# First products copied from bank to bank as the start of a second chain, block 6's first layer by seven products, left tokens in plane order, and a new order of the work

## The chip, the cores and the metric

The kernel runs on one core of a Trainium2 chip. A core has TensorE (PE in the profile; PEld is its weight load), VectorE (DVE), ScalarE (ACT), GpSimd (POOL) and SyncE (SP), which issues most transfers. They run at once, each in its own fixed order, and wait for each other through semaphores. SBUF is the working memory; PSUM, in eight banks, takes what matmuls put out. The metric is the device time of one execution in microseconds, lower is better.

## What is computed

```python
def _attn_ref(q, k, v):               # q, k, v: 8 x 8 x 576 x 64
    q_d, k_d, v_d = means over 4 neighbouring positions
    out_up = np.repeat(sm_attn(q_d, k_d, v_d), 4, axis=2)
    mask = np.abs(pos[:, None] - pos[None, :]) < 4
    out_local = softmax of the masked scores, times v
    return out_up + out_local

def _moe_ref(x, w_in, w_out):         # x: 4608 x 512; w_in: 512 x 2048; w_out: 2048 x 512
    h = x @ w_in
    g = h - np.tanh(h)
    return g @ w_out
```

The attention's output, 512 wide for each of 4608 tokens, goes through two dense layers with x - tanh(x) between them.

## The kernel before

**Tiling.** There are 8 batches ("blocks" 0 to 7) of 576 tokens. Attention works on pairs of heads, four pairs to a block, 32 pairs in all. A pair's queries and keys are loaded (`st`), cast (`qr`), turned, scored on PE with 64 rows (L691, L701, L707), put through exp on ACT (`E`), masked on DVE (L747), multiplied with the values (L761), normalized on DVE (`r` L777, `ln` L779), turned back and joined into `xT` (L797). A block's dense layers take 512 of its tokens; the other 64, the "left" ones, of two blocks at a time form groups of their own (`left1`, `left2`, `left_pair`).

**First layer.** For blocks 0 to 6 it is `mm1` (L838): for each of 16 chunks of the hidden width four matmuls of 128x512, tanh on ACT (L850), a subtract on DVE into `gT` (L853). For block 7 it is `first7`, a fast 2x2 scheme: seven products of quarters instead of eight, with sums of weights (`SS`, L872, in seats of `st`) and of tokens (`XS`, L883, in `rr` and `rT`), for four groups of chunks (L949). Each product has 16 matmuls of 128x256.

**Second layer.** For blocks 1 to 7 it is such a scheme too (`product`, L1277; seven products, with `token_sums` L1212 on DVE and `weight_sums` L1186). The products come in the order 1, 2, 6, 7, 4, 5, 3 (in block 7 another one). 1 and 2 accumulate in one bank, 6, 7 and 4 in a second, 5 and 3 in a third. A result that also needs product 1 gets it from SBUF: after product 1 ACT copies the bank to `keep` (L1298), and each of three results adds it: after product 6 and after product 7 a POOL add of `keep` to the copied result (L1348), after product 4 an add on DVE that also empties the bank (L1301). `first7` does the same with its own buffers `HK` (K0: copy L932, adds L939 on POOL or DVE, L971 on DVE).

**Left tokens.** After the tanh (L1003) DVE's subtract (L1005) reorders them from (column, group) to (group, column), token by token, so that a result's 64 rows can be stored in one run.

**Order.** No scheduler decides it. Each piece of work is recorded by `op` with what it reads and writes, and four tables fix the rest: `TURNS` the order in which all pieces are put out, `ENGINES` the engine where there is a choice, `BANKS` the PSUM bank of each chain, `BEHIND` which piece on DVE or POOL waits for one on the other. Each engine runs its pieces in that order. Banks 4 to 7 are called `DENSE`, all eight `TAIL`.

```python
        if n == 1:
            copy(full[0], kept(0))
        if n in (6, 7):
            dst, keys = (ra, yk(ya, 1)) if n == 6 else (rb, yk(yb, 1))
            copy(dst, keys)
            op("POOL", 1150, lambda: GP.tensor_tensor(
                out=dst, in0=dst, in1=full[0], op=ALU.add),
               reads=[("keep", 0)], writes=keys, port=True)
        if n == 4:
            plus(y[yb][:, :, 0:HD], full[0], ("keep", 0), yk(yb, 0))
```

Of the kernel before, what the change touches and what calls it, by code (L numbers as in the profile page):

```python
# [101 lines left out]
def kernel(  # L102
# [61 lines left out]
        "7f7C6R7g4y6h3b3c7D597E72887F6i8d8e5A5u7I6k7G71896l7l6m74758E8F7H8j736n6y76778k6z966o7J6K"  # L164
        "6L977K6I6J9C7L5i5j7m8K6p5q5r7M6w6x8L7N7r7O5o5p8p78CF6M6N9D79CC7s6u6v7x9f8Q6q6r7y9g6s6t8R"
        "9Z9I9a8S8q9T9b9cCG7z9h9i7X9jCE6O6P7Y7b9k7P7Q7Z9J9l9v9w7c6SCB8v9t9u7d8w9U7V7WCD9O8x9P7R7S"
        "7eAA9m9W7h9V9X9Y7i7a7n9QCH7o7j9nAB7p7k7t70ACAD809d9o9p849eAGAd7uA1A27qAe9q9zA0AH7vA79r81"
        "7T7U9sA8BD857w82ELEMAIAh9x9y86838AAgAJ8B878GAiAjCI8H8C8MAEAM8VAFATAU8I8NAVAW8DAm8WAKAbAc"
        "Ao8J8O8ZB0B18XAL8aBGBH8fAq8PAn8gAN8Y8bBFB2B38l8h8cA9ApAk8m8iBEAt8rAOBMBIBJ8sAP8n8yAr8z8o"
        "8tDt92BcBdBN908u93AXAYBAAl91DyIgIh989EBaBbAs9FBBENEO94CJBOBPBgBh99BQ9K95Dx9AAuBiDzE09G9L"  # L170
        "9BBqEaBKBrBLE39HA5A6CLCMEJEKAv9MBsAwE4B8B9BtBRBkBlByBTEb9NE5A3A4BjE6E7BzEcEdBSCREACSCKAQ"
        "8T8UE8C0E1C1CYARBUC6CZCoE2C7C8CpBVF8BWCuC9CAEgCvEHEIASAxD0EiIcIdAyBXEhEkD2AZAaBYDuD3BZB6"
        "B7AfF7EjAzD8EPEQElEVD9ERESEeDvBmEfIeIfBuE9BvF9FAEmDEBnEBBwFDB4B5DGEnBxDHFfEwExBoDMEXEYEC"
        "IFDNEDCXEWEuEvC2F2C3ETEUDSCaFEC4BpCbBCCgIGC5F3ChFVFWFeFFCmFGFgEEEFCNFICnCTFHCUFTFUDTFBFJ"
        "COFjFkCVCcFnCPCdEoCWF4F5DFCeDUEpDwCiCQD1CjFCG7G8EqDZG1G2DaCfFZCkCqFhFiCrClFoCwCsCxDfBeBf"
        "IHFKD4G3G4CtD5CyIKDiD6CzFpFaFqDAFrIJD7DBILIMG9DIFsJxDJEGDjDKFbFcDoFtEyEzFlDpDCDODLF0F1MU"
        "DPMVG5G6DqDVIwDQ9R9SDWDDIPDbErEsDRDXDcDkIQDdDYDlDrDsFLDeFRFSJRDmGJFXFYJSEZDnGOIkIlGTFuGH"
        "GUFmFvGIHhHmGZHrINGaGcIOGhGbGuFMGAGzF6FNIqGiFdH0FwFOFPEtFxH5IuGnHAIRJ1FyFzHCIVIvHDJ2ISHI"
        "IxIyGtHNITHwHSJ3GBGCIUGsHUIiIjFQJ4HVJTJUHaG0HfJ5IIIWJ6IsItGDJ7JKJLIXIrGEHgJkJlIzHTGKGFIY"
        "GLJGJHJ8ImInGMJXGGGPJEJFJ0GQJ9K0K1GNGVJYGWGRJAGdJyGXGeGSJzJZJVGfGYJMGjK2K3JbGkGgHBJaGoHx"  # L180
        "GpDgDhGlGvIZIaK6GwGqI0K7GxI5GmJNJmJnIAJWMWGyJBJCH1H2GrJdMYH6H7JcH3K8H8K4HEJsK9HFH9MZIBH4"
        "MeHGMaMbHJJeKAICK5HKJtHHIoIpHOMfHPJoJpJfHLJgHWNAKLKMKCHXIbJqJrHMHbHQHcMrMsHYHRHiJOJPKBHj"
        "HdHZKJKKMgHkHeHnJuJvMhHoJIJJHlHsMzN0HpKuHtRDREI1HuI2HqNBMcKDI3JDNCNDM4HvKZKaNGI4M5JhJiI6"
        "I7KEKFKRKbI8KwKSMdKcI9KGKHNHKxKhNhMiL2IDIEKvJwKiKPKQKjMkKNKOKkMjJQL3L9MAKpMlLANEKqKrLPNF"
        "MmKsKtOELQMnLVMvMwNgLWMtMuN5NILbN6MBJjNiNjNJLdKILeNKLjMxMyNMNLLkNVNWL8KVNmKTKUNNLpNnHyHz"
        "KWMXNOLBLqN1N2NPLrKXN7N8LCNkKYMoMpQmLHNlLIOCLsOLNQNRNoLNOMKdNpLOKlOFOGKmNqLxMGODKnKeLcNs"
        "LyKoMJKfM3ONNbKyKgOOL4NdNeNrKzOPOHOIMKNcL0OQL5NtL6L1NTNUO7LDN9NZNaNuLEO8L7O1O2LJMqORNvLK"
        "N3N4LFLRLSLLQnLGNwNxQrOSLTLMLXNSOJLYNzO0OTOKOUMPMQQwLULfOVOWLZLgMRLlQxLhLmLaUoLtLnLiQqLu"
# [35 lines left out]
    )  # L224
    BEHIND = (
        "0211 1H12 1D1V 0z20 1t2f 5I30 5Q5N 635B 5w5W 6562 6c2x 6d6A 5u6i AACD ABCH AmAF AnAL DxC"
        "J F8CZ FfFD DFFn MUFt GAGb IrJ6 JNK7 MZJs NBKu OELA LqNn ODLO O7OQ QoNy RYOp RNR1 SURu S"
        "VRd UqUs Q0S9 UtT7 RkVM U6Vm VuW1 WJWB WIWG WWWZ WjWr XGXc XtX8 Y3Y6 YHYL YwYx ZiZj"
    )

# [1297 lines left out]
```

## Time and profile before

| what | value |
|---|---|
| time of three runs, median (lowest to highest) | 309.29 us (308.97 to 310.74) |
| span of the profiled execution | 308.9 us |
| last DVE instruction (L1046) | starts at 305.20 us, 0.42 us long |
| granted TensorE clock | 1.000 |
| first-layer matmuls, L838, 128x512 | 448 |
| first-layer matmuls by products, L949, 128x256 | 112 |
| second-layer matmuls by products, L1277, 128x256 | 1120 |
| normalizations, L779 | 32, from 16.8 us to 253.9 us |

The profile lists for each group of instructions the line, the engine, the operation, what is written and read with its shape, the count, then the busy time in us, the mean of one in ns, and the idle time of the engine before them with what ended it. A row of a stretch gives the busy time of each engine within it. One matmul's own duration (379 ns for 128x512) is longer than the distance between two, since they overlap in the array; what a stage of matmuls takes follows from the distance.

### The profile page before, as it was taken

To read this page: it belongs to the slowest core of one execution; us is meant where nothing else is said; L and a number is where in the kernel's file an instruction comes from. 1 tells how busy PE (TensorE), PEld (TensorE's weight loads), DVE (VectorE), ACT (ScalarE), POOL (GpSimd) and SP (SyncE) were. 2 spreads that over 40 slices of the span, in tenths; PEclk is the share of its full clock that TensorE was granted. 3 is DMA by queue.
4 is the path that set the end of the run, shared out by engine and by line. 5 is a ranking of instruction groups with operands and counts; after the bars stand their busy time and mean duration, and the time that the engine had idled before them with its cause. 6 is when DMAs were issued, how large, how long until landed. Compare 5 with 4: busy or idle time off the path is not lost.

```text
span 308.9 us, 8018 instructions
## 1 busy us (share of the span) xinstructions
PE 297.2 (96%) x3052; PEld 205.1 (66%) x3052; DVE 266.7 (86%) x475; ACT 221.0 (72%) x395; POOL 166.4 (54%) x227
## 2 busy tenths in 40 slices
PE   7877999999999999999999999999999999999995
PEld 2655555545577755875577765656988656889984
DVE  2677788679998988999999888999999899989995
ACT  2768686279888786988958888888789666775410
POOL 5337657026864466337872278376344766466451
PEclk9999999999999999999999999999999999999999
DMA  7999999999999999899999999989999364001215
GB/s 228 235 246 235 241 241 172 217 209 247 242 242 284 244 222 259 234 172 294 176 270 222 287 217 181 280 222 268 175 223 210 57 111 161 2 3 55 94 42 156
DMA packets 121192, 60.84 MB, mean 197 GB/s; under 512 B 88896, under 2 KB 119104, under 8 KB 121152
## 3 DMA queue, kind: packets, MB, share of 16 engines
q1 hardware_dynamic: 115968, 55.27, 77.3%
q0 software_dynamic: 4224, 4.19, 8.5%
q10 hardware_dynamic: 960, 0.85, 1.0%
q8 instruction: 24, 0.39, 0.5%
q14 instruction: 16, 0.13, 0.1%
HBM read 44.04 MB, written 9.44 MB: 173 GB/s over the span
## 4 chain that ended last, share of the span: by engine, by line
PE 88%; SPq 4%; DMA 3%; DVE 2%; issue 1%; ACT 1%; ACTq 0%; DVEq 0%
PE ps L838 32%; PE ps L1277 27%; PE ps L761 5%; PE ps L992 5%; PE ps L1137 5%; PE ps L949 4%; PE ps L691 3%; PE ps L1109 2%; PE ps L1076 2%; SPq L406 2%; DMA sr<-in_q_dram 2%; DMA vst<-in_v_dram 1%; PE ps L707 1%; PE ps L804 1%; SPq L382 1%
## 5 line engine op out<-in xcount | busy, mean ns | idle before, releaser
L838 PE MATMUL ps<-xT,w_in_sb 128*128 128x512 bf16 x448 | 106.8, 379 | 0.0
L850 ACT ACTIVATE u<-ps 128x512 f32<-128x512 f32 x112 | 65.9, 600 | 24.7 <-PE ps L838 23.3
L853 DVE TENSOR_TENSOR gT<-ps,u 128x512 bf16<-128x512 f32 x112 | 74.6, 683 | 9.3 <-ACT u L850 8.1
L1277 PEld LDWEIGHTS <-gT 128*128 128x128 bf16 x672 | 64.5, 98 | 13.3 <-DVE gT L1212 0.4
L838 PEld LDWEIGHTS <-w_in_sb 128*128 128x128 bf16 x448 | 41.5, 98 | 41.3
L540 POOL CAST qr<-st 128x512 bf16<-128x512 f32 x42 | 25.3, 613 | 39.4 <-DVE Tw L1186 15.5
L1277 PE MATMUL ps<-w_out_sb,gT 128*128 128x256 bf16 x336 | 44.1, 273 | 0.0
L1277 PE MATMUL ps<-Tw,gT 128*128 128x256 bf16 x336 | 42.8, 273 | 0.2 <-DVE gT L1212 0.2
L712 ACT ACTIVATE E<-ps 128x912 bf16<-128x912 f32 x32 | 29.9, 934 | 2.5 <-PE ps L701 2.3
L779 DVE TENSOR_TENSOR ln<-ps,r 128x768 bf16<-128x768 f32 x32 | 30.5, 955 | 0.9
L618 ACT COPY kt<-kq 128x576 bf16<-128x576 bf16 x23 | 27.1, 1184 | 0.8 <-DMA kq<-qr 0.5
L1348 POOL TENSOR_TENSOR y<-y,keep 128x512 f32<-128x512 f32 x12 | 15.3, 1274 | 19.1 <-DVE E L747 6.3
L761 PEld LDWEIGHTS <-E 128*128 128x128 bf16 x576 | 21.5, 97 | 6.0 <-DVE E L747 0.8
L747 DVE TENSOR_TENSOR E<-E,mask 128x1152 bf16<-128x1152 bf16 x31 | 23.3, 758 | 2.5 <-ACT E L716 2.1
L720 ACT ACTIVATE E<-ps 128x576 bf16<-128x576 f32 x32 | 20.9, 653 | 2.7 <-PE ps L707 2.7
L628 POOL TENSOR_TENSOR half<-kq 128x576 f32<-128x576 bf16 x15 | 19.2, 1278 | 5.9 <-ACT u L850 3.5
L633 POOL TENSOR_TENSOR qkd<-half 128x288 bf16<-128x288 f32 x22 | 17.6, 798 | 4.5 <-DVE r L777 2.6
L761 PE MATMUL ps<-vw,E 128*128 128x65 bf16 x320 | 18.8, 193 | 0.9 <-DVE E L747 0.5
L1212 DVE TENSOR_TENSOR gT<-gT 128x2048 bf16<-128x2048 bf16 x14 | 17.2, 1227 | 0.7 <-PE ps L1277 0.5
L797 POOL TENSOR_TENSOR xT<-lT 128x336 bf16<-128x336 bf16 (+1 forms) x22 | 14.5, 683 | 4.3 <-DVE half L628 4.3
L992 PE MATMUL ps<-xT,w_in_sb 128*128 128x128 bf16 x256 | 16.6, 219 | 0.0
L761 PE MATMUL ps<-vpr,E 128*128 128x65 bf16 x128 | 16.3, 194 | 0.0
(184 smaller groups left out, 542.3 us busy)
## 6 DMA issues: line engine op xcount, KB each, us to landing
vst<-in_v_dram SPq DMA_DIRECT2D x56, 160.0 KB, 4.1
st<-in_q_dram SPq DMA_DIRECT2D x28, 256.0 KB, 3.8
st<-in_k_dram SPq DMA_DIRECT2D x28, 256.0 KB, 5.1
out_dram<-y SPq DMA_DIRECT2D x14, 512.0 KB, 3.7
v<-in_v_dram SPq DMA_DIRECT2D x20, 256.0 KB, 3.8
w_in_sb<-in_moe_w_in_dram POOLq DMA_DIRECT2D x4, 512.0 KB, 9.2
w_out_sb<-in_moe_w_out_dram POOLq DMA_DIRECT2D x4, 512.0 KB, 7.8
vr<-in_v_dram SPq DMA_DIRECT2D x8, 128.0 KB
```

The source lines that it names most:

```text
L540: (eng, ns, lambda dst=dst, src=src, fn=fn: fn(out=dst, in_=src), port)
L618: ("ACT", 1180, lambda: A.copy(out=ktv, in_=src), False),
L712: A.activation(out=E[s][:, :, E0:E0 + 456], in_=at(s1)[:, :, PS0:512], func=AF.Exp, scale=SCALE)
L720: A.activation(out=E[s][:, :, EP:EW].rearrange("p h (i c) -> p h i c", i=2)[:, :, :, 0:G], in_=at(s2)[:, :, 120:408].rearrange("p h (i c) ...
L747: eng.tensor_tensor(out=el, in0=el, in1=mask.unsqueeze(1).to_broadcast([128, 2, S]), op=ALU.mult)
L761: T.matmul(po[:, hh, 65 * n:65 * n + 65], E[s][:, hh, e:e + 128], vv, start=start, stop=stop)
L779: op("DVE", 960, lambda: V.tensor_tensor(out=ln[s].rearrange("p n (h d) -> p h n d", d=D), in0=blocks()[:, :, :, 0:64], in1=r[s].unsqueeze ...
L838: T.matmul(at(name)[:, 0, :], w_in_sb[:, dc, fc * 128:(fc + 1) * 128], xT[dc][:, c0:c0 + S].rearrange("p (c g) -> p c g", c=4)[:, :, 0:128 ...
L850: op("ACT", 600, lambda: A.activation(out=u[us], in_=at(name)[:, 0, :], func=AF.Tanh), reads=[("hd", kb, fc)], writes=[("u", us)], uses=[n ...
L853: op("DVE", 690, lambda: V.tensor_tensor(out=gT[g][:, fc, :], in0=at(name)[:, 0, :], in1=u[us], op=ALU.subtract), reads=[("hd", kb, fc), ( ...
L992: T.matmul(at(name)[:, 0, 128 * f:128 * f + 128], w_in_sb[:, dc, (f0 + f) * 128:(f0 + f) * 128 + 128], xT[dc].rearrange("p (b c g) -> p b ...
L1277: T.matmul(dst, left[:, f, 128 * j:128 * j + 128], right[:, f, :], start=(first and e == 0 and f == 0 and (j == 0 or apart)), stop=(e == 1 ...
```

## The change

Four things are changed.

1. *Product 1 as a seed.* In `first7` and, for blocks 1 to 6, in `product`, the bank of product 1 is copied into another PSUM bank (`seed`), and products 6, 7 and 4 accumulate on top of it. `keep`, K0 and all adds of them fall away there; after product 4 the bank is only copied out (in `product`), or taken by tanh and subtract directly (in `first7`). The seed's bank is one of 4 to 7; the half-wide chains of block 7 and of the left tokens go to banks 0 to 3 (`LOW`).
2. *Block 6 by seven products.* `first7` runs for blocks 6 and 7 (`FIRST7`). The weight sums are made once, for block 6. Its intermediate buffers are in seats of `vst`; as the sums use seats of `st`, `rr` and `rT`, block 6's dense work is recorded after all attention.
3. *Left tokens in plane order.* The subtract is plain; the stores write the 64 rows in steps of four.
4. *New tables* `TURNS`, `ENGINES`, `BANKS`, `BEHIND`. Copies after products may now be on DVE too.

```diff
+    HK = {NBLK - 2: [(old_v(0), old_v(1)), (old_v(2), old_v(3))],
...
-    def first7():
-
-        kb, g = NBLK - 1, (NBLK - 1) % 2
+    def first7(kb):
+
+        g = kb % 2
...
-                                    (1, SS[0], W[0][0], 1, 0), (3, W[0][1], SS[1], 1, 1)):
+                                    (1, SS[0], W[0][0], 1, 0),
+                                    (3, W[0][1], SS[1], 1, 1)) if kb == FIRST7[0] else ():
...
-                     6: (summed(1), [("ws", 1)], lambda k: cut(XS[1][:, k]), dk(1), 6, True),
+                     6: (summed(1), [("ws", 1)], lambda k: cut(XS[1][:, k]), dk(1), 6, False),
...
+            def seed(fn, G=G):
+                fn(out=at(("hz", kb, G, 6))[:, 0, :], in_=at(("hz", kb, G, 1))[:, 0, :])
...
                 if n == 1:
-                    copy(1, K0, [ka] + (k0 if G < 2 else []))
+                    op(None, 0, None, choice=[("ACT", 600, lambda seed=seed: seed(A.copy), False),
+                                              ("DVE", 690, lambda seed=seed: seed(V.tensor_copy), False, 0)],
+                       reads=[("hzd", kb, G, 1)], writes=[("hzd", kb, G, 6)],
+                       opens=(("hz", kb, G, 6), DENSE), uses=[("hz", kb, G, 1)])
...
-                if n in (6, 7):
-                    go = more(ra if n == 6 else rb)
-                    op(None, 0, None, choice=[("POOL", 1150, lambda go=go: go(GP), True),
-                                              ("DVE", 640, lambda go=go: go(V), True, 0)],
-                       reads=[ka], writes=[kc if n == 6 else kd])
                 if n == 4:
-                    op("DVE", 690, lambda G=G, K0=K0: V.tensor_tensor(
-                        out=K0, in0=at(("hz", G, 6))[:, 0, :], in1=K0, op=ALU.add),
-                       reads=[("hzd", G, 6)], writes=[ka], uses=[("hz", G, 6)])
-                    shrink(K0, [ka], 1, 0)
+                    shrink(None, [("hzd", kb, G, 6)], 1, 0, bk=6)
...
-        op("DVE", 1015, lambda: V.tensor_tensor(
-            out=to[:, f0:f0 + 4, :].rearrange("p f (b g c) -> p (f b) g c", b=2, c=4),
-            in0=at(name)[:, 0, :].rearrange("p (x c g) -> p x g c", c=4, g=16),
-            in1=u[us].rearrange("p (x c g) -> p x g c", c=4, g=16), op=ALU.subtract),
+        op("DVE", 690, lambda: V.tensor_tensor(
+            out=to[:, f0:f0 + 4, :].rearrange("p f n -> p (f n)"),
+            in0=at(name)[:, 0, :], in1=u[us], op=ALU.subtract),
...
-                       out=bass.AP(tensor=row.tensor, offset=row.offset + HD * c, ap=[[Dm, LEFT], [1, HD]]),
+                       out=bass.AP(tensor=row.tensor, offset=row.offset + HD * c,
+                                   ap=[[Dm, 4], [4 * Dm, LEFT // 4], [1, HD]]),
...
-        if n == 1:
+        if n == 1 and last:
             copy(full[0], kept(0))
+        elif n == 1:
+            more, keym = ("z", kb, 1), ("zd", kb, 1)
+
+            def seed(fn):
+                fn(out=at(more)[:, 0, :], in_=at(name)[:, 0, :])
+            op(None, 0, None, choice=[("ACT", 600, lambda: seed(A.copy), False),
+                                      ("DVE", 690, lambda: seed(V.tensor_copy), False, 0)],
+               reads=[key], writes=[keym], opens=(more, DENSE), uses=[name])
...
-            op("POOL", 1150, lambda: GP.tensor_tensor(
-                out=dst, in0=dst, in1=full[0], op=ALU.add),
-               reads=[("keep", 0)], writes=keys, port=True)
         if n == 4:
-            plus(y[yb][:, :, 0:HD], full[0], ("keep", 0), yk(yb, 0))
+            copy(y[yb][:, :, 0:HD], yk(yb, 0))
...
-            while made <= b:
+            while made <= b and (made < FIRST7[0] or b == NBLK - 1):
```

Line numbers move by a few: the first layer by products is L949 before and L954 after, the second layer L1277 and L1279, the weight sums L872 and L879, the token differences L883 and L890, the cast to `qr` L540 and L546, the normalization L779 and L785.

DVE, before, in the attention of the last pairs (`E` mask, `r` and `ln` of a pair, `gT_123` the first layer of block 6, `st_75` a weight sum):

```order
L777 RECIPROCAL r_116<-ps 128x12
L1301 TENSOR_TENSOR y_130<-ps,y_130 128x2x256
L779 TENSOR_TENSOR ln_118<-ps,r_116 128x2x6x64
L777 RECIPROCAL r_115<-ps 128x12
L779 TENSOR_TENSOR ln_117<-ps,r_115 128x2x6x64
L853 TENSOR_TENSOR gT_123<-ps,u_125 128x512
L853 TENSOR_TENSOR gT_123<-ps,u_127 128x512
L853 TENSOR_TENSOR gT_123<-ps,u_126 128x512
L872 TENSOR_TENSOR st_75<-w_in_sb 128x2048
L747 TENSOR_TENSOR E_114<-E_114,mask 128x2x576
```

and DVE at the corresponding place in the changed kernel:

```order
L1005 TENSOR_TENSOR gL<-ps,u_127 128x512
L546 COPY qr_93<-st_76 128x2x4x64
L879 TENSOR_TENSOR st_76<-w_in_sb,st_74 128x2048
L803 TENSOR_TENSOR xT_69<-lT_119 128x3x4x28
L803 TENSOR_TENSOR xT_69<-lT_119 128x2x4x30
L890 TENSOR_TENSOR rr_79<-xT_67 128x256
L890 TENSOR_TENSOR rr_80<-xT_69,rr_79 128x256
L890 TENSOR_TENSOR rT_81<-xT_69,xT_67 128x256
L803 TENSOR_TENSOR xT_70<-lT_120 128x3x4x28
L803 TENSOR_TENSOR xT_70<-lT_120 128x2x4x30
L890 TENSOR_TENSOR rr_79<-xT_68 128x256
```

The wide subtracts of block 6's first layer are gone from here; weight sums and token differences stand between the last casts and joins of the attention.

ACT, before, around product 1 of a second layer (`u` tanh, `keep` the copy):

```order
L716 ACTIVATE E_113<-ps 128x2x120
L712 ACTIVATE E_113<-ps 128x2x456
L1298 COPY keep_131<-ps 128x512
L850 ACTIVATE u_126<-ps 128x512
L850 ACTIVATE u_127<-ps 128x512
```

and in the changed kernel:

```order
L726 ACTIVATE E_113<-ps 128x2x2x144
L472 COPY vw_88<-vst_83 128x10x64
L1326 COPY ps<-ps 128x512
L718 ACTIVATE E_113<-ps 128x2x456
L856 ACTIVATE u_127<-ps 128x512
```

The copy stands in the same place between products 1 and 2, and writes a PSUM bank.

POOL, before, where results of a second layer get `keep` added (`y`), among sums for pooled keys (`half`, `qkd`):

```order
L628 TENSOR_TENSOR half<-kq_95 128x576
L482 TENSOR_TENSOR vp_110<-v_103 128x2x64
L1348 TENSOR_TENSOR y_130<-y_130,keep_131 128x2x256
L633 TENSOR_TENSOR qkd_100<-half 128x2x144
L1348 TENSOR_TENSOR y_128<-y_128,keep_131 128x2x256
```

and in the changed kernel:

```order
L634 TENSOR_TENSOR half<-kq_95 128x576
L546 COPY qr_93<-st_76 128x2x4x64
L488 TENSOR_TENSOR vp_110<-v_103 128x2x64
L634 TENSOR_TENSOR half<-kq_95 128x576
L639 TENSOR_TENSOR qkd_100<-half 128x2x144
```

All twelve adds of `keep` are gone from POOL; in all it has 197 rows instead of 223, and DVE 502 instead of 467.

More of the change, by code (lines that the diff above doesn't have):

```diff
@@ L1297, in copy @@
         def copy(out, writes):
[L1298 removed]
+            op(None, 0, None, choice=[
+                ("ACT", 600, lambda: A.copy(out=out, in_=pb()), False),
+                ("DVE", 690, lambda: V.tensor_copy(out=out, in_=pb()), False, 0)],
+               reads=[key], writes=writes, uses=[name])
         def plus(out, other, k0, writes):
             op("DVE", 690, lambda: V.tensor_tensor(out=out, in0=pb(), in1=other, op=ALU.add),
[L1302 removed]
+               reads=[key] + ([k0] if k0 else []), writes=writes, uses=[name])
         def add(out, m, other, k0, writes):
@@ L1407 @@
     TAIL = [(b,) for b in range(8)]
+    LOW = [(b,) for b in range(4)]
+    FIRST7 = (6, 7)
     CAST_V = [("POOL", 740, GP.tensor_copy, True), ("ACT", 740, A.copy, False),
```

186 lines of the change are left out of this document (93 added, 93 removed).

## The prediction

> **What bounds the kernel now.** I read the page's first part, then TensorE's waits, then busy time by stretch, then the chain of waits, then the groups of VectorE (DVE). The page gives each engine's busy time:
>
> ```profile
> span 308.9 us, 8018 instructions
> PE 297.2 (96%) x3052; PEld 205.1 (66%) x3052; DVE 266.7 (86%) x475; ACT 221.0 (72%) x395; POOL 166.4 (54%) x227
> ```
>
> A busy TensorE (PE) need not be the bound, so the second view asks what it waited for between 40 us and the end. One line answers, 0.2 us in all:
>
> ```profile
> PE ps L1277 <- DVE gT L1212: 0.2, 1, 0.2
> ```
>
> The third view cuts the span into the start, two long middle parts and the dense end. Columns: PE, weight loads, DVE, ScalarE (ACT), GpSimd (POOL), TensorE's granted clock, the DMA engines' share and their rate.
>
> ```profile
> 0.00:40.00 40.00, 32.24 (x393) 20.30 (x394) 26.92 (x80) 25.49 (x54) 22.08 (x42) 1.00 1.02 237
> 40.00:199.20 159.20, 159.20 (x1583) 102.15 (x1582) 141.25 (x245) 125.83 (x221) 85.95 (x121) 1.00 1.06 234
> 199.20:254.00 54.80, 54.65 (x607) 39.20 (x605) 50.41 (x83) 43.86 (x75) 31.03 (x42) 1.00 0.89 186
> 254.00:305.50 51.50, 51.16 (x475) 43.47 (x472) 47.98 (x70) 25.82 (x47) 27.30 (x25) 1.00 0.21 68
> ```
>
> From 40 us on PE has no gap to speak of and the clock is 1.00 in every row. So each matmul taken away is worth its whole issue time, as long as no other engine becomes the bound. The only one near is DVE: 92% busy from 199 to 254 us, 93% after that.
>
> **The matmuls.** The chain of waits shows runs of matmuls at full rate, one of the first layer's wide form and one of its narrow form (start, length, line, count):
>
> ```profile
> 253.62 5.18 PE ps L838 x24
> 270.14 2.62 PE ps L949 x24
> ```
>
> That is 5.18/24 = 0.216 us for 512 columns and 2.62/24 = 0.109 us for 256. Block 6's first layer was 64 wide ones, 13.8 us. Seven products over four groups are 112 narrow ones, 12.2 us. The difference is -1.6 us.
>
> The new order also changes how often PE goes over to the 64-row score matmuls and back: counted in its rows, 78 times before and 74 now. One such change in the timeline (start, length):
>
> ```profile
> 247.00 0.71 PE L1277 MATMUL ps<-w_out_sb,gT 128*128 128x256 bf16 x5
> 247.64 0.38 PE L691 MATMUL ps<-kq,kt 64*128 64x112 bf16 x8
> ```
>
> Five matmuls at 0.109 us end their issue at 247.55; the score matmul starts at 247.64, 0.09 us late. Four fewer changes give -0.4 us. PE's own path is thus shorter by 2.0 us.
>
> **The seeds.** Each first product was copied to SBUF by ACT and added to three later results. Now ACT copies it into the bank in which the second chain accumulates, 14 times. What goes and what stays:
>
> ```profile
> L1298 ACT COPY keep<-ps 128x512 f32<-128x512 f32 x7 | 4.2, 596 | 2.6 <-PE ps L1277 2.6
> L618 ACT COPY kt<-kq 128x576 bf16<-128x576 bf16 x23 | 27.1, 1184 | 0.8 <-DMA kq<-qr 0.5
> L720 ACT ACTIVATE E<-ps 128x576 bf16<-128x576 f32 x32 | 20.9, 653 | 2.7 <-PE ps L707 2.7
> L1348 POOL TENSOR_TENSOR y<-y,keep 128x512 f32<-128x512 f32 x12 | 15.3, 1274 | 19.1 <-DVE E L747 6.3 <-DVE qkd L633 4.6 <-DVE half L628 4.1
> L1301 DVE TENSOR_TENSOR y<-ps,keep 128x512 f32<-128x512 f32 x6 | 4.0, 674 | 0.3 <-PE ps L1277 0.3
> ```
>
> No row shows a copy from PSUM into PSUM. The bounds are 0.58 us (the quickest ACT row from PSUM, 653 ns for 576 elements, scaled to 512) and 1.18 us (the slowest ACT copy, of 576 elements). I take 0.60, by the copy that it replaces. No new wait arises: product 2 already waited for that copy, because it writes the same bank, and product 6 comes after product 2. What is queued behind product 2 is all of PE. In PE's rows eight to ten narrow matmuls, 0.87 to 1.1 us, stand between products 1 and 2 in the three tightest places, which just covers 0.6 us and a signal. I cost the seeds at nothing; at 1.18 us three places would miss cover by 0.3 to 0.5 us each, 1.5 us at most with a little for the others. [...]
>
> The twelve POOL adds (15.3 us) leave an engine that is 54% busy. That alone saves nothing, since PE did not wait for them.
>
> **DVE, where the saving can be lost.** Block 6's first layer in products needs four sums of weights, eight differences of tokens and eight adds; the weight sums already stood there for block 7, but now come earlier. The left tokens' subtract gets contiguous and should fall from 1028 to the 683 ns of the same size in plain order. Prices:
>
> ```profile
> L853 DVE TENSOR_TENSOR gT<-ps,u 128x512 bf16<-128x512 f32 x112 | 74.6, 683 | 9.3 <-ACT u L850 8.1
> L1005 DVE TENSOR_TENSOR gL<-ps,u 128x512 bf16<-128x512 f32 x4 | 4.1, 1028 | 0.6 <-ACT u L1003 0.5
> L925 DVE TENSOR_TENSOR gT<-ps,u 128x512 bf16<-128x512 f32 x4 | 2.7, 679 | 0.0
> L977 DVE TENSOR_TENSOR vst<-ps,vst 128x512 f32<-128x512 f32 x2 | 1.4, 682 | 0.3 <-ACT y L1298 0.3
> L883 DVE TENSOR_TENSOR rr<-xT 128x256 bf16<-128x256 bf16 x1 | 0.3, 277 | 0.0
> L872 DVE TENSOR_TENSOR st<-w_in_sb,st 128x2048 bf16<-128x2048 bf16 x1 | 1.4, 1448 | 0.0
> L872 DVE TENSOR_TENSOR st<-w_in_sb 128x2048 bf16<-128x2048 bf16 x2 | 2.4, 1215 | 0.0
> L628 DVE TENSOR_TENSOR half<-kq 128x576 f32<-128x576 bf16 x9 | 7.0, 783 | 0.0
> ```
>
> I weigh one stretch that both orders have: from the normalization (ln, L779) of the 25th pair to that of the 32nd. Its row, and the densest 20 us of DVE beside it:
>
> ```profile
> 202.45:253.87 51.42, 51.27 (x571) 36.95 (x570) 47.11 (x75) 40.97 (x71) 29.14 (x40) 1.00 0.89 186
> 243.60:263.60 20.00, 20.00 (x167) 12.62 (x166) 18.95 (x30) 13.17 (x24) 13.72 (x20) 1.00 0.46 110
> ```
>
> In DVE's order the stretch goes from 75 instructions to 88. Out go 8 wide subtracts (8 x 0.683), 2 adds of keep (2 x 0.674), one half (0.783), and 4 x 0.345 on the left tokens: 9.0 us. In come 4 subtracts (0.679), 4 adds (0.682), 8 differences (0.28), 2 weight sums (1.3 and 1.4) and six small ones (2.2 together): 12.6 us. Net +3.6 us by rows. Neighbouring rows overlap by some 0.08 us (47.11 us busy is less than the rows' sum), and 13 more rows take up to 1.0 back. DVE's work there becomes 47.1 + 2.6 to 3.6, say 50 us.
>
> PE's work there: 82 wide first-layer matmuls become 43, narrow ones go from 0 to 76, second-layer ones from 200 to 188: -8.4 + 8.3 - 1.3 = -1.4, so 51.4 - 1.4 = 50.0 us. The stretch is balanced to a hair. DVE would have to be busy all the time, and its densest 20 us had 18.95, that is 94.8%; PE was the bound there, so 94.8% is no ceiling. With DVE 100% busy nothing is handed back; at 94.8% the stretch takes 52.8 us, 2.8 us more than PE's own. I take 97.7%, about half way: 51.2 us, +1.2 us. What is late then is block 6's first products, behind the weight sums and differences.
>
> The rest costs nothing: the first 1105 rows of PE, 102 of DVE and 83 of ACT are the same, so the start is; the loads of the last k stand up to 8 us of PE's work later, and 7 us before their cast, against 5.1 us to landing on the page. After the 32nd normalization DVE has 75 instructions against 71, cheaper ones. The last transfers move the same 64 rows of 1 KB in another row order, behind the same last add.
>
> **Sum.** 308.9 - 1.6 - 0.4 + 1.2 = 308.1 us. The median of the runs, 309.29, is 0.4 above the profiled span; with that 308.5 us.
>
> **Rivals.**
> Faster: DVE works off its stretch without idling, or carries some sums into the lighter part behind. Then 0 to 0.4 us is handed back: 308.9 - 1.8 + 0.4 = 307.5. For it: emptier POOL. The weight sum L872 took 1448 ns once and 1215 otherwise, and POOL was 29.1 us busy in the stretch; ten such collisions fewer would give DVE 2.3 us and end the balance in PE's favour. Against it: only 0.2 us of waiting was left before, and more of PE's waits now stand close behind what ends them. [...]
>
> Slower: DVE becomes the bound of the stretch and keeps its old share there, 47.11/51.42 = 92%. Then 50 us of work take 54.6, 4.6 more than PE's, and the time is 308.9 - 2.0 + 4.6 + 0.4 = 311.9. It decides as soon as the stretch passes 53.5 us, a DVE share under 93.5%. For it: no 50 us of this profile has a higher share than 93%. Against it: DVE's idle time was waiting for ACT and PE, which ends when work queues up behind it.
>
> Seeds at 1.18 us: PE waits 1.5 us more, 308.5 + 1.5 = 310.0. For it is only that the form is unseen; against it all ACT copies of 512 f32 from PSUM at 0.59 to 0.60.
>
> **Chances.** A measurement tells some 0.5% from no change here, that is 307.7 to 310.8. My forecast (no difference beyond that) 0.38, the seeds' rival 0.07, both inside; the faster rival 0.35, the slower 0.20. So faster 0.35, same 0.45, slower 0.20. The forecast's own range is 307.7 to 309.7. The range for 8 in 10 takes in most of the faster rival and the near half of the slower: 306.8 to 311.5.
>
> **What would show it.** Right: the first layers of blocks 6 and 7 as 224 narrow matmuls; ACT's rows from PSUM to PSUM near 0.6 us; DVE over 95% busy between the two normalizations and PE waiting there for DVE by about 1 us, on first-layer products; left subtracts near 0.68 us. Wrong: waits of PE on ACT's seeds, PE gaps under 0.3 us in all (then the faster rival holds), or a DVE that is under 93% busy while PE waits (then the slower). Waits in the last 50 us or in the first 40, which I cost at nothing, would make the sum itself wrong.

## The result, and the profile after

| | before | changed |
|---|---|---|
| median of four runs each | 310.01 us (308.97 to 311.11) | 314.49 us (313.66 to 314.81) |
| ratio, 95% interval | | 1.0156 (1.0114 to 1.0199) |
| span of the profiled execution | 308.9 us | 312.8 us |

The change makes the kernel slower by about 4.5 us between the medians; 308.5 was forecast. Four views show where the time went. The page's first lines (busy time of each engine):

```profile
span 312.8 us, 8112 instructions
PE 297.8 (95%) x3100; PEld 210.1 (67%) x3100; DVE 270.0 (86%) x508; ACT 219.4 (70%) x395; POOL 150.1 (48%) x198
```

VectorE (DVE) works 3.3 us longer than before. TensorE (PE) is counted as busy 0.6 us longer, but this count also takes in time in which matmuls under way wait; what its own path costs is worked out in the last table. (The second layer has 336 + 336 + 112 = 784 matmuls of 128x256 in both kernels by the rows of the trace, where the table of the kernel before says 1120; no sum uses that figure.) The waits of PE from 40 us on, one line before, are now three (what waited, for what, us in total, times, longest):

```profile
PE ps L954 <- DVE xT L803: 0.9, 1, 0.9
PE ps L954 <- DVE gT L933: 0.4, 1, 0.4
PE ps L1077 <- DVE sr L1311: 0.2, 1, 0.2
```

This view counts only time in which the pipelined array stood empty. Counted as distance between neighbouring matmuls beyond the usual one, with gaps under 0.12 us left out, PE loses 0.75 us at 127 to 163 us, 2.2 us at 230 to 255 us and 1.2 us at 269 to 302 us: 4.2 us in all, where before had 0.3. That measure is used from here on.

The stretches, with the columns of the prediction's third view, and the time from the end of the last DVE add to the end of the span, which the prediction did not look at:

```profile
0.00:40.00 40.00, 33.52 (x399) 20.80 (x401) 28.07 (x81) 25.79 (x55) 22.90 (x44) 1.00 1.06 244
40.00:199.20 159.20, 158.94 (x1586) 102.36 (x1585) 141.95 (x260) 120.47 (x213) 78.53 (x103) 1.00 0.99 222
199.20:254.00 54.80, 53.67 (x620) 41.17 (x619) 53.35 (x94) 46.31 (x79) 27.54 (x37) 1.00 0.93 211
254.00:305.50 51.50, 50.78 (x500) 45.21 (x497) 45.47 (x73) 26.87 (x51) 21.13 (x18) 1.00 0.21 71
306.89:312.84 5.95, 0.00 (x0) 0.00 (x0) 0.00 (x0) 0.00 (x0) 0.00 (x0) 0.68 0.20 63
```

From 199 to 254 us DVE is 97% busy, against 92%, and PE falls short of the stretch by 1.1 us. And the last row: no engine works for 5.95 us, with the DMA engines at 0.20 of their capacity and 63 GB/s. The same piece of the kernel before:

```profile
305.62:308.94 3.32, 0.00 (x0) 0.00 (x0) 0.00 (x1) 0.00 (x0) 0.00 (x0) 0.97 0.46 132
```

So 2.6 of the 3.9 us between the two spans come after the last instruction of the computation. The view of the DMA for those two pieces, changed kernel first (share of 16 engines in 40 slices, in tenths; packets and rate):

```profile
DMA  2223222222312222223232232322110000000000
DMA packets 389, 0.37 MB, mean 63 GB/s; under 512 B 24, under 2 KB 389, under 8 KB 389
```
```profile
DMA  9999999899962049969993000000000000000000
DMA packets 509, 0.44 MB, mean 132 GB/s; under 512 B 80, under 2 KB 509, under 8 KB 509
```

Fewer bytes were left to write than before, in packets of the same 1 KB and the same mean 48 ns. But the share stands at two to three tenths where it was nine: counting packets in flight, four or five at a time for 3.9 of the 4.5 us that the data took, where before 14 to 17 flew for 1.2 of 1.9 us. Two queues were writing, and still only four or five packets flew.

### The profile page after: what moved, and what is told of

Same layout as the page of the kernel before. It is cut to its first block, busy times and chain, and to the rows that moved or that the text cites. A ratio compares the mean times of both kernels' runs of the same rounds, so it can differ in the third digit from the quotient of the medians.

```text
span 312.8 us, 8112 instructions
## 1 busy us (share of the span) xinstructions
PE 297.8 (95%) x3100; PEld 210.1 (67%) x3100; DVE 270.0 (86%) x508; ACT 219.4 (70%) x395; POOL 150.1 (48%) x198
## 5 line engine op out<-in xcount | busy, mean ns | idle before, releaser
L844 PE MATMUL ps<-xT,w_in_sb 128*128 128x512 bf16 x384 | 91.1, 379 | 0.0
L1279 PEld LDWEIGHTS <-gT 128*128 128x128 bf16 x672 | 64.0, 98 | 12.5 <-DVE gT L1214 0.4
L859 DVE TENSOR_TENSOR gT<-ps,u 128x512 bf16<-128x512 f32 x96 | 63.5, 684 | 9.9 <-ACT u L856 9.5
L856 ACT ACTIVATE u<-ps 128x512 f32<-128x512 f32 x96 | 55.6, 603 | 19.0 <-PE ps L844 16.9
L844 PEld LDWEIGHTS <-w_in_sb 128*128 128x128 bf16 x384 | 35.9, 98 | 36.7
L1279 PE MATMUL ps<-Tw,gT 128*128 128x256 bf16 x336 | 43.5, 273 | 0.1
L1279 PE MATMUL ps<-w_out_sb,gT 128*128 128x256 bf16 x336 | 43.4, 273 | 0.0
L634 POOL TENSOR_TENSOR half<-kq 128x576 f32<-128x576 bf16 x17 | 21.8, 1283 | 28.6 <-ACT y L1153 7.7
L546 POOL CAST qr<-st 128x512 bf16<-128x512 f32 x32 | 20.5, 648 | 28.9 <-DVE gT L1214 5.9
L785 DVE TENSOR_TENSOR ln<-ps,r 128x768 bf16<-128x768 f32 x32 | 30.6, 955 | 0.9
L753 DVE TENSOR_TENSOR E<-E,mask 128x1152 bf16<-128x1152 bf16 x31 | 24.5, 793 | 0.0
L639 POOL TENSOR_TENSOR qkd<-half 128x288 bf16<-128x288 f32 x21 | 16.7, 796 | 8.1 <-DVE half L634 4.1
L1301 ACT COPY y<-ps 128x512 f32<-128x512 f32 x21 | 12.4, 591 | 6.5 <-PE ps L1279 6.2
L992 PEld LDWEIGHTS <-w_in_sb 128*128 128x128 bf16 x256 | 15.3, 98 | 1.8
L767 PE MATMUL ps<-vp,E 128*128 128x65 bf16 x128 | 16.3, 192 | 0.1
```

Source lines behind the costliest of these rows:

```text
L634: eng.tensor_tensor(out=half, in0=flat[:, 0:576], in1=flat[:, 576:1152], op=ALU.add)
L753: eng.tensor_tensor(out=el, in0=el, in1=mask.unsqueeze(1).to_broadcast([128, 2, S]), op=ALU.mult)
L767: T.matmul(po[:, hh, 65 * n:65 * n + 65], E[s][:, hh, e:e + 128], vv, start=start, stop=stop)
L785: op("DVE", 960, lambda: V.tensor_tensor(out=ln[s].rearrange("p n (h d) -> p h n d", d=D), in0=blocks()[:, :, :, 0:64], in1=r[s].unsqueeze ...
L844: T.matmul(at(name)[:, 0, :], w_in_sb[:, dc, fc * 128:(fc + 1) * 128], xT[dc][:, c0:c0 + S].rearrange("p (c g) -> p c g", c=4)[:, :, 0:128 ...
L856: op("ACT", 600, lambda: A.activation(out=u[us], in_=at(name)[:, 0, :], func=AF.Tanh), reads=[("hd", kb, fc)], writes=[("u", us)], uses=[n ...
```

## The experiments

The time of a run is 1.7 to 1.8 us above its span in the kernel before and 1.9 to 2.0 in the changed one. These 0.2 us lie outside everything that the profile shows; the reordered kernels e9 to e14 do not have them, and why was not looked into. In the profiled executions the 500th matmul, up to which the orders are nearly the same, starts between 49.3 and 50.9 us. Spans of single executions therefore differ by up to 1.6 us for no reason of the change, and medians are compared. Ratios and intervals are those on record, not quotients of the medians beside them.

| kernel | median us | before us | ratio (95%) |
|---|---|---|---|
| e1 rows 16 by 4 | 312.33 | 309.59 | 1.0085 (1.0058 to 1.0112) |
| e2 token order again | 315.64 | 309.59 | 1.0179 (1.0137 to 1.0220) |
| e3 before, plane order alone | 314.50 | 309.59 | 1.0145 (1.0107 to 1.0183) |
| e4 short masks | 312.69 | 309.59 | 1.0092 (1.0060 to 1.0123) |
| e5 before, plane order, rows 16 by 4 | 309.10 | 309.66 | 0.9998 (0.9971 to 1.0025) |
| e6 before, masks twice | 311.89 | 309.66 | 1.0074 (1.0044 to 1.0103) |
| e7 read in token order | 365.20 | 309.66 | 1.1809 (1.1757 to 1.1861) |
| e8 before, read in token order | 362.68 | 309.66 | 1.1721 (1.1675 to 1.1767) |
| e9, e10 reordered | 330.78, 330.24 | 309.75 | 1.0672, 1.0665 (1.0635 to 1.0706) |
| e11 kept apart | 323.79 | 309.59 | 1.0445 (1.0400 to 1.0491) |
| e12 few moves | 309.39 | 309.44 | 0.9989 (0.9962 to 1.0016) |
| e13 more room | 309.41 | 309.86 | 0.9991 (0.9972 to 1.0009) |
| e14 more room, b | 307.97 | 309.86 | 0.9936 (0.9912 to 0.9959) |

### The stores: e1, e2, e3, e5

e1 changes only the order in which the stores walk the rows:

```diff
-                                   ap=[[Dm, 4], [4 * Dm, LEFT // 4], [1, HD]]),
+                                   ap=[[4 * Dm, LEFT // 4], [Dm, 4], [1, HD]]),
```

> The changed kernel, in which the stores of the left tokens walk the rows of the output as 16 by 4 in place of 4 by 16: the same 64 rows of 1 KB, so the left tokens' rows land at each other's places; nothing else is touched. Theory A (a store is dealt out to the DMA engines by its outermost dimension, so that 4 by 16 keeps 4 of 16 busy): the stretch from the last add's end to the end of the span, 5.9 us in the changed kernel, goes back to about the 3.3 us of before, and the time falls by 2.6 us to about 311.9; TensorE's waits stay at about 4.2 us. Rival B (rows in steps of four are slow for the memory, whatever their order): the same rows, so 314.5 as it was.

It took 312.33 us, and the piece after the last add is as short as before:

```profile
307.55:310.88 3.33, 0.00 (x0) 0.00 (x0) 0.00 (x0) 0.00 (x0) 0.00 (x0) 1.00 0.37 85
```

The waits of PE stayed (4.0 us). Theory A's numbers hold: the rows' places in the output do not matter here, the outermost dimension of the store does (3.33 us with 16, 5.95 with 4). With 16 there, 14 to 17 packets were in flight again for 1.0 of the 1.9 us that the data took.

What the trace shows is packets in flight: four or five with 4 outermost, 14 to 17 with 16. In the changed kernel one queue alone had four or five (306.89 to 307.31 us), and two queues together hardly more, six at most and for 0.17 us. The trace does not name the engines: that the store is dealt out to 4 of 16 of them is theory A's reading, and was not shown.

e3 makes the change of the left tokens alone, in the kernel before:

```diff
-        op("DVE", 1015, lambda: V.tensor_tensor(
-            out=to[:, f0:f0 + 4, :].rearrange("p f (b g c) -> p (f b) g c", b=2, c=4),
...
+        op("DVE", 1015, lambda: V.tensor_tensor(
+            out=to[:, f0:f0 + 4, :].rearrange("p f n -> p (f n)"),
+            in0=at(name)[:, 0, :], in1=u[us], op=ALU.subtract),
...
-                       out=bass.AP(tensor=row.tensor, offset=row.offset + HD * c, ap=[[Dm, LEFT], [1, HD]]),
+                       out=bass.AP(tensor=row.tensor, offset=row.offset + HD * c, ap=[[Dm, 4], [4 * Dm, LEFT // 4], [1, HD]]),
```

> The kernel before, with the left tokens in plane order alone (subtract in plain order, stores 4 by 16). Theory A: the end gets 2.6 us longer, VectorE 5.5 us of work less of which TensorE feels at most its one wait of 0.3 us: 310.0 + 2.6 - 0.3 = 312.3. Rival B (the left tokens have nothing to do with it): 310.0 or up to 0.3 us less. Rival C (a lighter VectorE lets the order run ahead more): under 309.5.

314.50 us, 2.2 more than theory A gave. The piece after the last add grew by 3.4 us, not 2.6 (583 packets of 1 KB fall into it here, 369 in the changed kernel), and a new wait of 1.4 us stands at 171 us. These are the end, PE's one wait after 40 us, and ScalarE's (ACT's) row that it waited for (start, length, in brackets its idle time and what ended it):

```profile
305.43:312.15 6.72, 0.00 (x0) 0.00 (x0) 0.00 (x0) 0.00 (x0) 0.00 (x0) 0.67 0.31 87
```
```profile
PE ps L1276 <- ACT keep L1297: 1.3, 1, 1.3
```
```profile
172.39 0.58 ACT L1297 COPY keep<-ps 128x512 f32<-128x512 f32 x1 [2.55 <-DMA out_dram<-keep]
```

`left2` stores its results from `keep`, and the next product's copy overwrites `keep`. A store with 4 outermost reads it for so long that the copy (ACT idle for 2.55 us until that store is done), and with it product 2 and all of PE behind it (1.3 us in the view), waits. The changed kernel is spared this because product 1 no longer goes to `keep`: two parts of the change meet here.

e5 is e3 with the rows 16 by 4:

> The kernel before with plain left subtracts and the left tokens' rows stored 16 by 4 (they land at each other's places in the output), to stand beside the same with 4 by 16, which took 314.5 us, 4.9 more than before: 3.4 us at the end and a wait of 1.4 us at 171 us of ScalarE's copy to keep, for a store that still read keep. Theory A (both are the price of stores on 4 DMA engines): the end is 3.3 us as before, the wait at 171 us is gone, and the time is 309.6 (309.2 to 309.9; VectorE's 5.5 us less of work are not felt, since TensorE has only 0.3 us of waits to lose). Rival B (the plain order, or VectorE running earlier, makes the wait at 171 us): end 3.3 us, wait still over 1 us, 311.

309.10 us, ratio 0.9998: the end is 3.3 us, the wait at 171 us is gone, PE has no wait at all after 40 us. So plane order by itself and the 5.5 us less on DVE make no difference that can be told (the interval is 0.3% to either side), and what e3 lost, 314.50 against 309.10 us, was the price of stores with 4 outermost.

e2 is the reverse, the changed kernel with the left tokens' part undone (strided subtract, stores of 64 rows in a run):

> The changed kernel with the left tokens in token order again: the reordering subtract (16 of them, 0.35 us longer each) and stores of 64 rows in one run. Theory A (the stores cost 2.6 us at the end): 311.9 less or more what the longer subtracts add; four of them lie in the stretch in which VectorE has no idle time, so up to 1.4 us there, 312 to 313.3. Rival B (the left tokens have nothing to do with the end): 314.5 or more, since VectorE only gets more work.

315.64 us is rival B's time, though the end is theory A's; its interval overlaps the changed kernel's, so the two can't be told apart. The end is 3.3 us again, but PE's waits rose from 4.2 to 7.1 us: sixteen subtracts 0.35 us longer are 5.5 us for DVE, and 2.9 of them reached PE. My expectation counted four of the sixteen; a full DVE passes on work from the other stretches too.

### DVE's load: e4, e6

e4 shortens the mask of the last eight pairs, e6 puts it on twice for five pairs of the kernel before (the mask is 0 or 1):

```diff
 def do_mask(eng):
+    n = 64 if p >= 24 else S
-    eng.tensor_tensor(out=el, in0=el, in1=mask.unsqueeze(1).to_broadcast([128, 2, S]),
-                      op=ALU.mult)
+    eng.tensor_tensor(out=el[:, :, 0:n], in0=el[:, :, 0:n],
+                      in1=mask[:, 0:n].unsqueeze(1).to_broadcast([128, 2, n]), op=ALU.mult)
```
```diff
 def do_mask(eng):
-    eng.tensor_tensor(...)
+    for _ in range(2 if p in (26, 27, 28, 29, 30) else 1):
+        eng.tensor_tensor(...)
```

> The changed kernel, with the mask of the last eight pairs on 64 of 576 columns only, which leaves the rest unmasked and takes about 0.6 us from each of eight VectorE instructions between 200 and 255 us. Theory A (VectorE is full there, and TensorE's 2.3 us of waits between the 25th and the 32nd normalization come from its amount of work): those waits shrink to under 0.5 us and the time falls by 1.8 us or more, to about 312.5; the waits at 269, 300 and 302 us and the end stay. Rival B (the waits come from single places where the order puts long VectorE work ahead of what TensorE needs next, not from the amount): the wait of 1.0 us at 239 us stays above 0.6 us and the time falls by less than 1 us.

> The kernel before with the mask of pairs 27 to 31 put on twice, which gives VectorE five more instructions of 0.75 us, 3.4 to 3.7 us, between the 25th and the 32nd normalization, about what the change adds there (47.1 to 50.4 us busy), with TensorE's work and the order untouched. Theory A (the amount of VectorE's work against TensorE's decides): VectorE had 4.0 us idle there, so TensorE waits for it 0.5 to 2.3 us, and the time is 310.1 to 311.9. Rival B (the changed order, not the amount, makes TensorE wait): less than 0.4 us of waits and 309.6 to 309.9.

e4 took 312.69 us, 1.8 less than the change (the intervals of the two ratios overlap slightly, so the reading rests on the waits below); e6 311.89, 2.2 more than before. The stretch from the 25th to the 32nd normalization, in the changed kernel, in e4 and in e6:

```profile
202.77:254.63 51.86, 50.73 (x597) 39.74 (x596) 50.37 (x90) 43.30 (x76) 25.63 (x35) 1.00 0.92 209
```
```profile
201.93:251.77 49.84, 49.76 (x597) 39.70 (x596) 45.92 (x89) 43.35 (x77) 25.82 (x35) 1.00 1.08 218
```
```profile
201.69:255.04 53.35, 52.29 (x572) 37.12 (x571) 51.19 (x80) 41.10 (x71) 28.72 (x40) 1.00 0.83 179
```

With 45.9 us of work for DVE the stretch takes 49.84 us, which is what PE needs (50.0 was forecast), and PE's waits fall from 2.2 to 0.25 us, the one of 1.0 us at 239 us among them. With 51.2 us put on DVE in the old order, PE waits 2.0 us, where it waited 0.3. So both theories A hold: less work on DVE takes PE's waits away in the changed order, and more work makes them in the old one. Whether another order does better is asked further below. The longest wait shows the mechanism. DVE (start, length) and PE at 239 us in the changed kernel:

```profile
236.87 0.44 DVE L546 CAST qr<-st 128x512 bf16<-128x512 f32 x1
237.40 1.23 DVE L879 TENSOR_TENSOR st<-w_in_sb,st 128x2048 bf16<-128x2048 bf16 x1
238.54 0.52 DVE L803 TENSOR_TENSOR xT<-lT 128x336 bf16<-128x336 bf16 x2
238.98 0.28 DVE L890 TENSOR_TENSOR rr<-xT 128x256 bf16<-128x256 bf16 x1
239.30 0.29 DVE L890 TENSOR_TENSOR rr<-xT,rr 128x256 bf16<-128x256 bf16 x1
239.51 0.28 DVE L890 TENSOR_TENSOR rT<-xT,xT 128x256 bf16<-128x256 bf16 x1
239.71 0.52 DVE L803 TENSOR_TENSOR xT<-lT 128x336 bf16<-128x336 bf16 x2
```
```profile
239.14 0.27 PE L954 MATMUL ps<-xT,w_in_sb 128*128 128x256 bf16 x1
240.28 0.92 PE L954 MATMUL ps<-xT,w_in_sb 128*128 128x256 bf16 x7 [0.87 <-DVE xT L803]
```

Block 6's product 1 waits for the second join of tokens (239.71), which stands behind a weight sum of 1.23 us and three token differences, without a gap between them.

### A dead end: e7, e8

To have plain subtracts and stores of 64 rows in a run, e7 lets PE read the left tokens in token order, with a step of 144 elements inside; e8 does it in the kernel before.

```diff
-                             xT[dc].rearrange("p (b c g) -> p b c g", b=NR, c=4)[:, s0:s0 + 2, :, 128:G],
+                             xT[dc].rearrange("p (b c g) -> p b g c", b=NR, c=4)[:, s0:s0 + 2, 128:G, :],
```

> The changed kernel with the left tokens brought into token order by TensorE's first-layer matmuls, which read them from xT with a stride of 144 elements instead of in runs of 16; the subtract stays plain, and the stores are 64 rows in one run. All of the output is right. Theory A (the stores were the price, and a strided moving operand costs TensorE nothing): 312.3 us like the kernel with rows 16 by 4, end 3.3 us, L992 matmuls at the same distance (0.056 us). Rival B (TensorE reads a strided operand more slowly): the 256 matmuls take up to twice as long, 14 us more, 326; in between if the slowdown is partial.

> The kernel before with the same: TensorE reads the left tokens in token order, the subtract is plain, the stores are unchanged. Theory A (VectorE's 5.5 us less of work are hidden, as TensorE waits for VectorE only once, 0.3 us): 309.3 to 309.6, no difference that can be told. Rival B (a strided moving operand is slower on TensorE): up to 14 us more. Rival C (VectorE's relief shortens the start or the end too): under 309.

365.20 and 362.68 us: rival B, and with some 53 us nearly four times its bound of 14. The rows of those matmuls in e7 and in the changed kernel (shortest, median and longest in ns):

```profile
L992 PE MATMUL ps<-xT,w_in_sb x256: 377/400/408, 82.6 to 340.5; 128*128 128x128 bf16 x128
```
```profile
L992 PE MATMUL ps<-xT,w_in_sb x256: 218/219/230, 82.8 to 290.7; 128*128 128x128 bf16 x128
```

The distance between two of them is the price. In e7 24 stood in a row (start, length):

```profile
86.64 5.52 PE L992 MATMUL ps<-xT,w_in_sb 128*128 128x128 bf16 x24
```

That is (5.52 - 0.40)/23 = 0.223 us each, against 0.057 us in the changed kernel. 256 x 0.166 = 42 us; the other 11 us were not broken down. The granted clock was 0.92 in e7 and 1.00 in e1.

### The order: e9 to e14

What remained was to ask whether the change's matmuls are a gain at all when PE does not wait. These six kernels have all matmuls of the changed one. The last two groups of left tokens are in token order again, with stores of 64 rows in a run, and the tables put pieces elsewhere from 108 us on (e13, e14: from 52 us).

```diff
+        def less():
+            if m < NBLK // 2 - 2:
+                V.tensor_tensor(out=to[:, f0:f0 + 4, :].rearrange("p f n -> p (f n)"),
+                                in0=at(name)[:, 0, :], in1=u[us], op=ALU.subtract)
+            else:
+                V.tensor_tensor(
+                    out=to[:, f0:f0 + 4, :].rearrange("p f (b g c) -> p (f b) g c", b=2, c=4),
...
-                                   ap=[[Dm, 4], [4 * Dm, LEFT // 4], [1, HD]]),
+                                   ap=[[Dm, LEFT], [1, HD]]),
```

The new places were worked out from the durations in the changed kernel's trace, first as if DVE and GpSimd (POOL) did not disturb each other.

> The changed kernel, reordered by hand-made tables: from 108 us on, pieces of work stand in another order and 115 pieces with a choice of engine sit on another one, so that VectorE's work falls on GpSimd and ScalarE where these were idle and each piece comes before TensorE needs it; the left tokens of the last two groups are in token order again (eight subtracts 0.35 us longer, the last stores in one run), those of the first two stay in plane order. All matmuls are as in the changed kernel. Theory A (the change loses by VectorE's load and by the last stores alone, its matmuls are worth 1.8 us): TensorE's waits after 40 us fall from 4.2 to under 0.7 us, the end is 3.3 us, and the time is 309.6 - 1.8 + 0.1 to 0.7 = 307.9 to 308.5. Rival B (more work on GpSimd slows VectorE down as fast as it relieves it): waits of over 2 us, 309.8 or more.

> The same with another order of the same kind (107 pieces on another engine). Theory A: 307.9 to 308.5, TensorE's waits under 0.7 us. Rival B: 309.8 or more. If the two differ by over 1 us, it is single places that decide and not the amount of work.

330.78 and 330.24 us, rival B and far beyond it: DVE had 33 instructions fewer (475) and was 17 us longer busy (287.1). The masks (L747 before, L753 in the changed kernel, L752 in e9), and one of them in e9 beside POOL:

```profile
L747 DVE TENSOR_TENSOR E<-E,mask 128x1152 bf16<-128x1152 bf16 x31 | 23.3, 758 | 2.5 <-ACT E L716 2.1 <-ACT E L712 0.3
```
```profile
L753 DVE TENSOR_TENSOR E<-E,mask 128x1152 bf16<-128x1152 bf16 x31 | 24.5, 793 | 0.0
```
```profile
L752 DVE TENSOR_TENSOR E<-E,mask 128x1152 bf16<-128x1152 bf16 x27 | 25.5, 947 | 1.2 <-ACT E L721 1.2
...
259.48 1.82 DVE L752 TENSOR_TENSOR E<-E,mask 128x1152 bf16<-128x1152 bf16 x1
```
```profile
259.37 1.32 POOL L633 TENSOR_TENSOR half<-kq 128x576 f32<-128x576 bf16 x1
```

The mask starts 0.11 us after POOL's sum and ends 0.61 us after the sum's end (260.69): alone it takes 0.75. All eleven long masks of e9 show the same: each starts inside a POOL instruction that reads SBUF, 0.38 to 1.21 us before its end, and each ends 0.60 to 0.62 us after that end, however long the overlap. That reads as a mask which stands still until POOL is done, not as one that runs more slowly throughout. One that started first, at 109.26 us, took 746 ns, and there POOL's instruction ended late: `vp` took 845 ns, against some 460 undisturbed. Over all of DVE's instructions in e9, the time beyond what each form takes when it is quick (its tenth percentile) adds up to 34 us, nearly all of it beside POOL; in the changed kernel it is 9 us. The subtract from PSUM into `gT` (96 in e9, 682 ns on average) shows nothing of the kind: it has a median of 681 ns beside POOL and 679 ns without.

e11 was laid out so that such instructions do not meet:

> As the two reordered kernels (330 us, where VectorE's instructions that read and write SBUF only got up to twice as long while GpSimd was in one of its own: the mask 749 ns alone, up to 1825 beside GpSimd), but with an order in which such instructions of the two engines do not meet. Matmuls, left tokens and stores are as in those two. Theory A (the 22 us came from these meetings alone; the change itself loses by VectorE's load and the last stores): the mask's mean is under 800 ns, TensorE's waits after 40 us are under 1.5 us, the end is 3.3 us, and the time is 309.6 - 1.8 + 0.1 to 1.2 = 307.9 to 309.0. Rival B (moving pieces to GpSimd costs TensorE more than it brings whatever the order): over 310.

323.79 us, so theory A's time and its condition both failed: meetings were left (the masks' mean is 858 ns, the longest still 1.82 us, and DVE's time beyond the quick one is 24 us). So e11 does not decide between theory A and rival B. My reading, which no run tests, is that the first pieces on DVE ran later on the chip than planned, the next ones met POOL, and each meeting moved the following ones.

e12 therefore moves little, about 110 of 1,747 pieces and 14 to another engine, and only moves that also pay when all durations vary by some per cent:

> The changed kernel with few pieces moved: of 1,747 pieces on TensorE, VectorE, ScalarE and GpSimd about 110 stand elsewhere in their engine's order and 14 on another engine, chosen so that VectorE's and GpSimd's instructions within SBUF do not meet even when all runs some per cent late; the left tokens of the last two groups in token order with plain stores at the end, as in the other reordered kernels. Theory A (what the change loses is VectorE's work standing ahead of what TensorE needs, waits of 4.2 us, and the stores at the end, 2.6 us): waits under 1.5 us, the end 3.3 us, the time 307.9 to 309.3, below before's 309.6. Rival B (waits come back wherever VectorE is full, since its amount of work is the same or larger): waits over 2.5 us, 310.3 or more.

309.39 us: as fast as before (0.9989), 5 us faster than the change. Time and waits (1.9 us) lie between theory A and rival B, nearer to A, and the end is 3.6 us. Two waits were left, 0.8 us at 86 us and 1.1 us between 220 and 240 us. e13 and e14 give PE's needs some 0.3 us more room:

> Of the kernel with few moves (309.4 us, as fast as before), with some 40 more moves (140 of 1,747 pieces displaced against the changed kernel, 19 on another engine), from 52 us on, so that more of what TensorE needs is done 0.3 us ahead. Theory A (what was left there, waits of 0.8 us at 86 us and 1.1 us between 220 and 240 us, was single places, and the fewer matmuls are a gain once TensorE doesn't wait): waits under 0.8 us in all, the time 307.6 to 308.7. Rival B (with VectorE full the waits only move; before's time is what can be had): waits again about 2 us and 309.2 or more.

> The same from another start (122 pieces displaced, 19 on another engine). Theory A: 307.6 to 308.7, waits under 0.8 us. Rival B: 309.2 or more, waits of about 2 us.

e13 stayed at 309.41 us: rival B's time, but with about 1.0 us of waits and an end of 3.6 us, so that neither theory has it right. e14 took 307.97, 0.64% faster than before (the interval, 0.9912 to 0.9959, leaves out 1), with 0.3 us of waits from 200 us on. Its first lines, the stretch of before's third view and the one from the 25th to the 32nd normalization (13 matmul records of 128x512 are missing from the traces of e12 to e14; the weight loads, 3100, are all there):

```profile
span 306.6 us, 8102 instructions
PE 294.5 (96%) x3087; PEld 210.1 (69%) x3100; DVE 268.7 (88%) x497; ACT 220.1 (72%) x400; POOL 156.0 (51%) x204
...
199.20:254.00 54.80, 54.80 (x644) 43.08 (x642) 53.76 (x93) 48.35 (x84) 32.22 (x41) 1.00 1.00 217
202.46:252.27 49.81, 49.81 (x597) 39.75 (x596) 48.97 (x85) 43.42 (x77) 28.12 (x37) 1.00 1.00 211
```

PE has no idle time in a stretch in which DVE is 98% busy. Theory A holds for e14: it is 1.9 us faster than before, which is what the saved matmuls promised (1.8 us of PE's own path, next section). But e14 is not the changed kernel in another order alone. From the 25th to the 32nd normalization DVE has 85 instructions and 49.0 us of work, where the changed kernel has 90 and 50.4, and POOL has 2.5 us more. PE needs 49.8 us there, so no order that leaves all 50.4 us on DVE in this stretch could have been free of waits; with 49.0 this one is. e13 shows how little room there is: in the profiled executions it differs from e14 by 0.7 us of waits and 0.3 us of the end. That is 1.0 of the 1.4 us between their medians; the rest, and why e13's end is longer, were not looked into.

## Why the prediction was wrong, point by point

From the profiled executions, PE's own time taken from its 500th matmul to its last, less waits (253.6 us before, 251.9 after):

| term | forecast | measured |
|---|---|---|
| PE's own path (block 6's matmuls, fewer switches) | -2.0 | -1.8 |
| waits between the 25th and 32nd normalization | +1.2 | +1.9 (2.2, less before's 0.3) |
| waits elsewhere | 0 | +2.0 (0.75 and 1.2) |
| after the last add | 0 | +2.6 |
| sum | -0.8 | +4.7 |

The spans differ by 3.9, since the first 500 matmuls took 0.8 us less in that execution of the changed kernel. The medians of the runs differ by 4.5.

**The step that failed** is one sentence: "The last transfers move the same 64 rows of 1 KB in another row order, behind the same last add." Bytes and packets were right, and the price was not in them. The term was put at nothing, and it measured 2.6 us: with an outermost dimension of 4 the store kept four or five packets in flight instead of 14 to 17, with the DMA engines at 0.20 of their capacity at the end, where before had 0.46 and e1 0.37. With it the forecast's "The rest costs nothing" fell. It was not the only step. e1, which takes this price away, still needs 312.3 us, and the range ended at 311.5; the waits of the next two points are most of the rest. No store of the kernel before has such a small outermost dimension, so no row could price it.

**The mis-sized term** is DVE's. The mechanism was right: the stretch is balanced to a hair, DVE becomes full, block 6's first products wait behind weight sums and differences. The work was 50.4 us against 50, DVE's share of 51.86 us 97.1% against 97.7%, PE's work 49.8 (e4) against 50.0. Three small errors of 0.2 to 0.4 us with one sign made 2.2 us of waits out of 1.2. A balance between two engines magnifies what is wrong on either side. That 97.7% came so near owes something to luck: it was taken half way between 100% and "its densest 20 us had 18.95", but DVE's densest 20 us of the kernel before are those from 194.9 us on, with 19.35 us (96.8%). Half way from there is 98.4%, which gives 50.8 us and a wait of 0.8, further off.

**Waits outside the stretch** (2.0 us) were costed at nothing. "After the 32nd normalization DVE has 75 instructions against 71, cheaper ones" counted work over the whole rest; at 269 us three token sums of 3.1 us together stand ahead of one subtract that PE needs. e14, with pieces in other places and some on other engines, has no wait of this kind after 127 us but the 0.3 us named above, so the change does not force these waits. What made the 0.75 us before 163 us was not followed up.

**Right were** the seeds, which cost nothing: PE never waited for one, and the copies from bank to bank took 584 and 572 ns where 0.60 us was taken:

```profile
L946 ACT COPY ps<-ps 128x512 f32<-128x512 f32 x8 | 4.7, 584 | 1.2 <-PE ps L954 1.0
L1326 ACT COPY ps<-ps 128x512 f32<-128x512 f32 x6 | 3.4, 572 | 3.0 <-DVE gL L1005 2.3 <-PE ps L1279 0.6
```

The left subtracts (683 ns on average), the 224 narrow matmuls and the first wait's place came as described. The form of the sum was careless in one place: "The median of the runs, 309.29, is 0.4 above the profiled span" set the span of a long execution beside the median. A run's time is 1.7 to 1.8 us above its own span, so that execution took about 310.7; the difference to before was not touched by it.

**The rivals.** The slower one had the right engine, and its 311.9 us is near what the change takes without the price of its stores (e1, 312.3), but by a share of 92% that DVE did not have. The faster one hoped for less contention with a POOL that is busy for 16 us less; the masks grew from 758 to 793 ns instead. Eight of them lie beside POOL for over 0.2 us, with a median of 912 ns; before seven did, with a median of 747. In e9 it was not how busy POOL is that counted, but whether its instruction came first: a mask of 0.75 us then took up to 1.82.

## What to carry to other kernels

Before a transfer is called free, read the outermost dimension of its pattern: the same 64 rows of 1 KB with 4 outermost instead of 16 cost 2.6 us at the end (5.95 us against e1's 3.33), and 1.4 us in the middle where the next writer of the buffer waited (e3). Where one engine's saving is another's work, compare both over the same stretch, and take the outcome as uncertain by the errors of both. A saving is worth what the order lets through: the same matmuls made 314.5, 309.4 and 308.0 us, and moving work to an engine with time to spare made 330 where instructions of the two on SBUF met (e9).

## What was not expected of the hardware

A moving operand read with a step of 288 bytes makes a matmul of 128 columns take 0.223 us instead of 0.057, four times as long (e7), while runs of 16 elements (32 bytes) cost nothing that shows (0.057 is about half the 0.109 of 256 columns). The difference is 0.166 us on 128 columns.

Two queues with such stores kept four or five packets in flight together, at 63 GB/s in the end piece, where one alone had as many, so the second queue brought nothing that shows. And in e9 a mask that started inside a POOL instruction on SBUF ended only behind it: 0.75 us alone became up to 1.82, and all eleven long ones ended 0.60 to 0.62 us after POOL's end.
